# Gated mix of two attention blocks: the order of a pass over four rounds, with five bursts of V products

## The chip, the cores and the metric

The kernel runs on one core of a Trainium2 chip. The metric is device time in microseconds, the median of repeated executions of the same program. A profiled execution gives, beside its time, a trace with every instruction's engine, line, start and length. PE is the matrix engine (TensorE; its weight loads are listed as PEld), DVE is VectorE, ACT is ScalarE, POOL is GpSimd, and SP issues most of the transfers.

## The reference

Two attention blocks A and B read the same x (2048 tokens, 512 features). Each has 32 heads of 16 features and is a full softmax over 2048 keys. Their results are mixed by a gate per token. All inputs are float32.

```python
qkv = (x @ wqkv) -> q, k, v of 32 heads with Dh = 16
scores = einsum("bhqd,bhkd->bhqk", q, k) * (Dh ** -0.5)
p = softmax(scores)
o = einsum("bhqk,bhkd->bhqd", p, v) -> (2048, 512) @ wo

g = sigmoid((x * gate_w).sum(-1))
return g * A(x) + (1 - g) * B(x)
```

So there are 64 heads in all, each with a 2048 x 2048 matrix of scores, which is where the time goes.

## The kernel before

A prologue projects x to q, k and v, splits q and k into a high and a low part, and leaves them in DRAM. The main loop then works in *rounds*: a round is one head and one block of 128 keys, so a head has 16 rounds (NT) and there are 1024 (ROUNDS). The order of all instructions is written out by hand; nothing reorders them (`manual_schedule`). Every engine takes its own instructions in the order in which the program names them.

For each round there are four kinds of work:

- `score(r, c)`, a step "e": a matmul of 128 keys by 512 queries (50 rows of q and k parts, the maximum of each query among them) into a bank of the PSUM pool `ps_st` (four banks), then an exponential on ACT into a quarter of the tile `p` of that round (pool `ppool`, three buffers). Four of them make a round.
- the maxima, 20 rounds ahead (NT + LEAD): `max_plain(m, c)`, a step "m", is a matmul of 128 queries by 512 keys into the pool `ps_m` (three banks) and a maximum over it on DVE. For every second round, `max_rise` ("D": a matmul into `ps_st` and a Relu on ACT) and later `max_pair` ("A": a matmul into `ps_m` and one DVE instruction that adds the rise and takes the maximum) do in one DVE pass what two plain steps would do.
- `attend_next(n)`, a digit in the string: a *burst* of V products. The unit is a quarter, 128 of the 512 query columns of each of the four chunks of `p`. `attend` issues four matmuls at a time, one for each chunk, each at its own 32 columns of the array, and they add up in the one bank `acc`. Each takes 128 x 17 weights (V and a column of ones, which gives the denominator). A burst that crosses a round's end is two calls. Behind the last round of a head ACT copies `acc` out (`ev`), and the next head's first product waits for that.
- once a head, `max_split` reduces the maxima over the four chunks on DVE (`mrow`) and splits them on POOL; `max_rows` transposes them on DVE (`mt`), sends them out by one DMA on SP (`md`) and back by two into two rows of the head's q, on which the first "e" of that head waits.

The score matmuls ("e", "m", "D", "A") use 48 or 50 of the array's rows, and the helper `rows()` puts them by turns on partitions 0 and 64, so that two run at a time. `turn[0] = 0` at each burst starts again with partition 0.

The order comes from one string for each pass over two rounds, `FULL`; the last 20 rounds, which have no maxima left to take, use `LATE`. Work that is due by round (loads of V and weights, normalising, projections of finished groups of heads) stands in `later`; a pass calls what is due in its two rounds before its string begins, and projections wait for the next burst. The bursts run 8 quarters, two rounds, behind the scores.

Of the kernel before, what the change touches and what calls it, by code (L numbers as in the profile page):

```python
# [37 lines left out]
NT = S // P  # L38
# [5 lines left out]
ROUNDS = NH * NT  # L44
LEAD = 4
# [6 lines left out]
def gated_mha(ctx: ExitStack, tc: tile.TileContext, xT, x, wqkv_a, wo_a, wqkv_b, wo_b, gate_w, out):  # L52
# [34 lines left out]
    def load_stacks(h, halves=HALVES):  # L87
        dma = nc.sync.dma_start
        s, hh = divmod(h, H)
        g, j = divmod(hh, HG)  # L90
        q, k = q_st[h % 3], k_st[h % 3]
        qs, ks, xs = qd[s][g], kd[s][g], xd[s][g]

        def pairs(t, step, n=S):
            v = t[0, j]
            return bass.AP(tensor=v.tensor, offset=v.offset, ap=[[n, DH], [step, 2], [1, n]])

        for b in halves:
            dma(k[b:b + 32].bitcast(F32), pairs(ks, HG * DH * S))
            dma(q[b:b + 32].bitcast(F32), pairs(qs, 0))  # L100
            dma(k[b + 32:b + 48].bitcast(F32), ks[0, j])
            dma(q[b + 32:b + 48].bitcast(F32), qs[1, j])
        if h and halves[-1] == HALVES[1]:
            x = x_st[h % 2]
            dma(x[:32].bitcast(F32), pairs(xs, HG * DH * 512, 512))
            dma(x[32:SC].bitcast(F32), xs[0, j])
# [3 lines left out]


    LOWEST = -3.4028234e38
    FIRST = NT + LEAD + 2
    mxp, rises = {}, {}
    turn = [0]

    def rows():
        turn[0] ^= 1
        return HALVES[1 - turn[0]]

    def scores_bank(m, c):
        h, t = divmod(m, NT)
        if h not in mxp:
            mxp[h] = small.tile([P, NT, 4], F32, name="mxp")
            if h:
                pool.memset(mxp[h][:, FIRST % NT if h == 1 else 0::2, 1:2], LOWEST)
        pool_ = ps_st if c == "rise" else ps_m
        ps = pool_.tile([P, 512], F32, name="ps_st" if c == "rise" else "ps_m")
        b = rows()
        q = q_st[h % 3]  # L130
        if c == "rise":
            assert b == 0
            k = x_st[h % 2][:]
        else:
            k = k_st[h % 3][b:b + SC, c * 512:(c + 1) * 512]
        pe.matmul(ps, q[b:b + SC, t * P:(t + 1) * P], k, start=True, stop=True)  # L136
        return ps, mxp[h][:, t]

    def max_plain(m, c):
        ps, o = scores_bank(m, c)  # L140
        dve.tensor_reduce(o[:, c:c + 1], ps, op=ALU.max, axis=AX.X)  # L141
# [3 lines left out]
    def max_rise(m):  # L145
        ps, _ = scores_bank(m, "rise")
        rises[m] = small.tile([P, 512], F32, name="rise")
        act.activation(rises[m], ps, AF.Relu)  # L148

    def max_pair(m):  # L150
        ps, o = scores_bank(m, 0)
        rise = rises.pop(m)
        dve.tensor_tensor_reduce(out=rise, in0=ps, in1=rise, scale=1.0, scalar=LOWEST,  # L153
                                 op0=ALU.add, op1=ALU.max, accum_out=o[:, 0:1])
# [3 lines left out]
    def max_split(h):  # L158
        parts = mxp.pop(h)
        m = small.tile([P, NT], F32, name="mrow")  # L160
        mp = small.tile([P, 2, NT], F32R, name="mparts")
        dve.tensor_reduce(m, parts, op=ALU.max, axis=AX.X)  # L162
        pool.tensor_copy(mp[:, 0], m)  # L163
        pool.tensor_tensor(mp[:, 1], m, mp[:, 0].bitcast(F32), op=ALU.subtract)
        mparts[h] = mp

    def max_rows(h):
        mt = small.tile([P, 32], F32, name="mt")
        dve.transpose(mt, mparts.pop(h).rearrange("p i t -> p (i t)").bitcast(F32))
        q = q_st[h % 3]  # L170
        r = md[h % 3]
        nc.sync.dma_start(r.rearrange("i (t a x) -> a (i t) x", a=4, x=32), mt)
        for b in HALVES:
            nc.sync.dma_start(q[b + SC:b + SC + 2].bitcast(F32), r)
# [13 lines left out]
    with tc.tile_pool(name="xs", bufs=1) as xs, tc.tile_pool(name="pro", bufs=2) as pro, \  # L188
# [97 lines left out]
        ahead = [(m, c) for m in range(NT + LEAD) for c in range(4)]  # L286
# [228 lines left out]
    later = {}  # L515
# [53 lines left out]
    def attend(r, qa, qb):  # L569
        h, kt = divmod(r, NT)  # L570
        v, j = vg[h // HG], h % HG
        p = pt[r]
        final = h == NH - 1
        a = kt % 4
        first, last = (a == 0, a == 3) if final else (kt == 0, kt == NT - 1)
        for c in range(NQ):
            pe.matmul(acc[32 * c:32 * c + 17, qa * P:qb * P], v[:, 4 * a + c if final else kt, j],  # L577
                      p[:, c * 512 + qa * P:c * 512 + qb * P], start=first and qa == 0, stop=last,
                      tile_position=(0, 32 * c), skip_group_check=True)
        if qb < 4:  # L580
            return
        del pt[r]
        if final and last:
            ev = work.tile([P, 512], F32, name="ev")
            act.copy(ev, acc)  # L585
            hi = work.tile([P, 512], F32R, name="ev_hi", tag="num")
            lo = work.tile([P, 512], F32R, name="ev_lo")
            pool.tensor_copy(hi, ev)
            pool.tensor_tensor(lo, ev, hi.bitcast(F32), op=ALU.subtract)
            tail[kt // 4] = (hi, lo)  # L590
        elif last:
            G, j = divmod(h, HG)
            ev = work.tile([P, 512], F32, name="ev")
            act.copy(ev, acc)
            nc.sync.dma_start(od[G][j].rearrange("c r t -> (c r) t"), ev)


    done = [0]

    def attend_next(n):  # L600
        while n:
            r, qa = divmod(done[0], 4)
            qb = min(4, qa + n)
            attend(r, qa, qb)
            done[0] += qb - qa
            n -= qb - qa

    def score(r, c):
        h, kt = divmod(r, NT)
        if c == 0:  # L610
            pt[r] = ppool.tile([P, S], F32, name="p")
        q, k = q_st[h % 3], k_st[h % 3]
        kk, cc = (4 * (kt % 4) + c, kt // 4) if h == NH - 1 else (kt, c)
        b = rows()
        ps = ps_st.tile([P, 512], F32, name="ps_st")
        pe.matmul(ps, k[b:b + SC + 2, kk * P:(kk + 1) * P], q[b:b + SC + 2, cc * 512:(cc + 1) * 512],  # L616
                  start=True, stop=True)
        act.activation(pt[r][:, c * 512:(c + 1) * 512], ps, AF.Exp, scale=SCALE)  # L618
# [1 line left out]

    FULL = "m3memeem3meAe2Dmeee"
    LATE = "e2ee2ee2ee2e"
    after = {}

    for r in range(0, ROUNDS, 2):
        h, kt = divmod(r, NT)
        projects = []
        for rr in (r, r + 1):  # L630
            for fn, a in later.pop(rr, ()):
                if fn is project_out:
                    projects.append(a)
                else:
                    fn(*a)
        if kt == 0 and h + 2 < NH:
            load_stacks(h + 2)
        m = r + NT + LEAD
        plain = [(m, 2), (m, 3)] + [(m + 1, c) for c in range(4)]
        scored = 0  # L640
        for step in FULL if m < ROUNDS else LATE:
            if step == "e":
                score(r + scored // 4, scored % 4)
                scored += 1
            elif step == "m":
                max_plain(*plain.pop(0))
            elif step == "D":
                if m + 2 < ROUNDS:
                    max_rise(m + 2)
            elif step == "A":  # L650
                if m in rises:
                    max_pair(m)
                else:
                    max_plain(m, 0)
                    max_plain(m, 1)
            else:
                for a in projects:
                    project_out(*a)
                projects = []
                turn[0] = 0  # L660
                if r:
                    attend_next(int(step))
                if scored > 2 and r in after:
                    max_rows(after.pop(r))
        m += 1
        if m < ROUNDS and m % NT == NT - 1:
            max_split(m // NT)
            after[r + 2] = m // NT
    attend_next(8)
    fill_only.append(True)  # L670
    for fn, *a in fill:
        fn(*a)
# [25 lines left out]
```

## Time and profile before

| | us |
|---|---|
| median of 3 runs | 2805.46 (2804.55 to 2805.68) |
| profiled execution | 2804.7 |
| its span | 2802.9 |
| PE busy | 2785.4 |
| ACT busy | 2419.9 |
| DVE busy | 2363.9 |
| POOL busy | 254.8 |

The main loop fills the span from about 350 us on. A row of the timeline has the start in us from the span's start, the length in us, the engine, the line, the operation, the tiles (out<-in) and a count where like instructions in a row are merged. The end of a matmul is modelled, so the distance between starts says more than a length. A row of a group has the busy time and the mean length in ns of one, and then the engine's idle time before them with what ended it.

### The profile page before, as it was taken

The page shows a single profiled execution, that of the slowest core. Times are in us where ns is not written, and L with a number is a line of the kernel's source. Part 1 is how long each engine was busy: PE and PEld are TensorE (multiplying, and loading weights), DVE is VectorE, ACT ScalarE, POOL GpSimd, SP SyncE. Part 2 cuts the span into 40 slices and gives each one's busy share as a digit, 9 for nine tenths or more (in the row PEclk, how much of TensorE's full clock was granted, in tenths as well). Part 3 has the DMA queues.
Part 4 walks back from the last instruction along what each step waited for, and adds up shares of the span by engine and source line. Part 5 has one row for each costly group of instructions (what it writes and reads, how often), then busy time and mean ns, then how long its engine had stood idle before and what let it go on. Part 6 is the DMA issues. An engine that isn't in the chain of part 4 may idle for free.

```text
span 2802.9 us, 65443 instructions
## 1 busy us (share of the span) xinstructions
PE 2785.4 (99%) x26176; PEld 1319.3 (47%) x26176; DVE 2363.9 (84%) x4399; ACT 2419.9 (86%) x4758; POOL 254.8 (9%) x456
## 2 busy tenths in 40 slices
PE   8999999999999999999999999999999999999998
PEld 6877444444444444444444445444444444444444
DVE  4145799999999999999999877899999999998884
ACT  3221699999999999999999977899999999998785
POOL 2010111110000000000100232000000001011201
PEclk9999999999999999999999999999999999999999
DMA  7673333333332233333432442332333333333302
GB/s 255 206 251 145 84 62 78 69 70 59 70 62 53 50 58 62 58 60 58 89 54 50 104 100 63 58 56 49 63 54 60 58 78 70 58 73 86 77 10 92
DMA packets 91125, 225.24 MB, mean 80 GB/s; under 512 B 24150, under 2 KB 34358, under 8 KB 78278
## 3 DMA queue, kind: packets, MB, share of 16 engines
q1 hardware_dynamic: 88262, 212.15, 33.9%
q0 software_dynamic: 2560, 8.91, 1.2%
q8 instruction: 206, 3.38, 0.6%
q14 instruction: 97, 0.79, 0.1%
HBM read 152.07 MB, written 68.94 MB: 79 GB/s over the span
## 4 chain that ended last, share of the span: by engine, by line
PE 97%; DMA 1%; ACT 1%; DVE 1%; issue 0%; SPq 0%; DVEq 0%
PE acc L577 38%; PE ps_m L136 25%; PE ps_st L616 13%; PE ps_st L136 8%; PE ps_pro L233 5%; PE ps_m L459 3%; PE ps_pro L265 3%; ACT p L618 1%; DMA raw<-in_xT 0%; DMA k_st<-kd 0%; DMA qd<-part 0%; DVE mxp L141 0%; PE ps_st L459 0%; PE ps_st L510 0%; PE ps_m L510 0%
## 5 line engine op out<-in xcount | busy, mean ns | idle before, releaser
L618 ACT ACTIVATE p<-ps_st 128x512 f32<-128x512 f32 x4096 | 2077.0, 625 | 88.5 <-PE ps_st L616 73.8
L141 DVE TENSOR_REDUCE mxp<-ps_m 128x1 f32<-128x512 f32 x3094 | 1957.3, 683 | 183.4 <-PE ps_st L616 130.1
L136 PE MATMUL ps_m<-k_st,q_st 48*128 48x512 f32 x3595 | 1359.7, 446 | 1.2 <-DVE mxp L141 0.4
L616 PE MATMUL ps_st<-q_st,k_st 50*128 50x512 f32 x4096 | 1218.1, 427 | 0.0
L577 PE MATMUL acc<-p,vg 128*17 128x384 f32 (+1 forms) x16368 | 1186.0, 384 | 2.9 <-ACT ev L585 2.0
L136 PEld LDWEIGHTS ps_m<-k_st,q_st 48*128 48x128 f32 x3595 | 610.9, 184 | 555.4 <-DVE mxp L141 480.8
L616 PEld LDWEIGHTS ps_st<-q_st,k_st 50*128 50x128 f32 x4096 | 618.9, 185 | 198.6 <-ACT p L618 179.4
L577 PEld LDWEIGHTS acc<-p,vg 128*17 128x17 f32 x16368 | 315.1, 96 | 422.8 <-issue 400.0
L153 DVE CUSTOM_DVE_ANT_0 rise<-ps_m,rise 128x512 f32<-128x512 f32 x501 | 341.4, 681 | 0.0
L148 ACT ACTIVATE rise<-ps_st 128x512 f32<-128x512 f32 x501 | 301.7, 602 | 36.6
L136 PE MATMUL ps_st<-x_st,q_st 48*128 48x512 f32 x501 | 249.1, 497 | 0.0
L163 POOL CAST mparts<-mrow 128x16 fp32r<-128x16 f32 x64 | 12.6, 197 | 2010.9 <-DVE mrow L162 2010.9
L136 PEld LDWEIGHTS ps_st<-x_st,q_st 48*128 48x128 f32 x501 | 91.8, 183 | 211.8 <-ACT p L618 211.4
L237 ACT CAST part<-ps_pro 128x1024 fp32r<-128x1024 f32 x32 | 32.5, 1014 | 134.6 <-PE ps_pro L233 113.5
L238 DVE TENSOR_TENSOR part<-ps_pro,part 128x1024 fp32r<-128x1024 f32 x32 | 39.2, 1225 | 100.8 <-ACT part L237 82.0
L459 PE MATMUL ps_m<-wo,ot 128*128 128x512 f32 (+1 forms) x354 | 91.0, 402 | 0.0
L268 ACT COPY v_st<-ps_pro 128x512 f32<-128x512 f32 x31 | 18.2, 587 | 77.8 <-PE ps_pro L265 74.1
L233 PE MATMUL ps_pro<-xh,whi 128*128 128x512 f32 x256 | 72.9, 404 | 8.5 <-ACT xh L219 8.1
L459 PEld LDWEIGHTS ps_m<-wo,ot 128*128 128x128 f32 (+1 forms) x354 | 64.0, 188 | 20.2 <-issue 3.9
L233 PE MATMUL ps_pro<-xh,wlo 128*128 128x512 f32 x256 | 69.5, 394 | 0.0
L233 PE MATMUL ps_pro<-xl,whi 128*128 128x512 f32 x256 | 69.3, 393 | 0.0
L233 PEld LDWEIGHTS ps_pro<-xh,whi 128*128 128x128 f32 x256 | 47.5, 190 | 24.8 <-ACT xh L219 11.3
(99 smaller groups left out, 808.4 us busy)
## 6 DMA issues: line engine op xcount, KB each, us to landing
k_st<-kd SPq DMA_DIRECT2D x128, 256.0 KB
q_st<-qd SPq DMA_DIRECT2D x128, 256.0 KB
qd<-part SPq DMA_DIRECT2D x32, 512.0 KB
kd<-part SPq DMA_DIRECT2D x32, 512.0 KB
k_st<-kd SPq DMA_DIRECT2D x128, 128.0 KB
q_st<-qd SPq DMA_DIRECT2D x128, 128.0 KB
od<-ev SPq DMA_DIRECT2D x63, 256.0 KB
vd<-v_st SPq DMA_DIRECT2D x32, 272.0 KB
```

The lines of the kernel that those rows point to most:

```text
L136: pe.matmul(ps, q[b:b + SC, t * P:(t + 1) * P], k, start=True, stop=True)
L141: dve.tensor_reduce(o[:, c:c + 1], ps, op=ALU.max, axis=AX.X)
L148: act.activation(rises[m], ps, AF.Relu)
L153: dve.tensor_tensor_reduce(out=rise, in0=ps, in1=rise, scale=1.0, scalar=LOWEST, op0=ALU.add, op1=ALU.max, accum_out=o[:, 0:1])
L233: pe.matmul(ps[:, c * 512:(c + 1) * 512], a[:, k], b[:, k], start=n == 0, stop=n == 3 * KC - 1)
L237: act.copy(pt[0], ps)
L238: dve.tensor_tensor(pt[1], ps, pt[0].bitcast(F32), op=ALU.subtract)
L265: pe.matmul(ps[:, :DM], a[:, k, o:o + P], b[:, k], start=n == 0, stop=n == 3 * KC - 1)
L459: pe.matmul(ps, ot[a][:n, slot, sl], wt[b][:n, g], start=G == groups[0] and i == 0, stop=G == groups[-1] and i == 2)
L577: pe.matmul(acc[32 * c:32 * c + 17, qa * P:qb * P], v[:, 4 * a + c if final else kt, j], p[:, c * 512 + qa * P:c * 512 + qb * P], start=fi ...
L616: pe.matmul(ps, k[b:b + SC + 2, kk * P:(kk + 1) * P], q[b:b + SC + 2, cc * 512:(cc + 1) * 512], start=True, stop=True)
L618: act.activation(pt[r][:, c * 512:(c + 1) * 512], ps, AF.Exp, scale=SCALE)
```

## The change

A pass now covers four rounds, and `FULL` is a string for four: 16 "e", 12 "m", 2 "A", 2 "D", and five bursts of 3, 4, 3, 3 and 3 quarters. Twice the old string had six bursts (3, 3, 2, 3, 3, 2). Both "D" stand at the end of the pass and are for the rounds m + 4 and m + 6, so two rises are kept until the next pass. The first "m" of a pass is the third of its round. What is due by round is still called every two rounds: for the third and fourth round of a pass it is called ahead of the ninth "e". The bursts now run 7 quarters behind, as in the first pass those ahead of the eighth "e" are left out. `max_split` no longer stands at the end of a pass; it follows the first burst of the next one, and `max_rows` the second. `LATE` is the old string twice.

```diff
-    FIRST = NT + LEAD + 2
+    FIRST = NT + LEAD + 4
...
-    FULL = "m3memeem3meAe2Dmeee"
-    LATE = "e2ee2ee2ee2e"
-    after = {}
-
-    for r in range(0, ROUNDS, 2):
+    FULL = "mme3emmeem4meeemAe3emmeeem3meeemA3DeD"
+    LATE = "e2ee2ee2ee2e" * 2
+    splits = {}
+
+    for r in range(0, ROUNDS, 4):
...
+        due(r)
         if kt == 0 and h + 2 < NH:
             load_stacks(h + 2)
         m = r + NT + LEAD
-        plain = [(m, 2), (m, 3)] + [(m + 1, c) for c in range(4)]
+        plain = [(m + i, c) for i in range(4) for c in range(2 - i % 2 * 2, 4)]
+        pairs = [m, m + 2]
+        ahead = [m + 4, m + 6]
         scored = 0
+        steps = [max_split, max_rows] if r in splits else []
         for step in FULL if m < ROUNDS else LATE:
             if step == "e":
+                if scored == 8:
+                    due(r + 2)
                 score(r + scored // 4, scored % 4)
...
-                if r:
+                if r or scored >= 8:
                     attend_next(int(step))
-                if scored > 2 and r in after:
-                    max_rows(after.pop(r))
-        m += 1
-        if m < ROUNDS and m % NT == NT - 1:
-            max_split(m // NT)
-            after[r + 2] = m // NT
-    attend_next(8)
+                if steps:
+                    steps.pop(0)(splits[r])
+        if m < ROUNDS and (m + 4) % NT == 0:
+            splits[r + 4] = m // NT
+    attend_next(4 * ROUNDS - done[0])
```

More of the change, by code (lines that the diff above doesn't have):

```diff
@@ L618, in score, with due @@
         act.activation(pt[r][:, c * 512:(c + 1) * 512], ps, AF.Exp, scale=SCALE)
-    FULL = "m3memeem3meAe2Dmeee"
-    LATE = "e2ee2ee2ee2e"
-    after = {}
-    for r in range(0, ROUNDS, 2):
+    FULL = "mme3emmeem4meeemAe3emmeeem3meeemA3DeD"
+    LATE = "e2ee2ee2ee2e" * 2
+    splits = {}
+    for r in range(0, ROUNDS, 4):
         h, kt = divmod(r, NT)
         projects = []
[L630 to L635, printed above, removed]
+        def due(first):
+            for rr in (first, first + 1):
+                for fn, a in later.pop(rr, ()):
+                    if fn is project_out:
+                        projects.append(a)
+                    else:
+                        fn(*a)
+        due(r)
         if kt == 0 and h + 2 < NH:
@@ L647, in gated_mha @@
             elif step == "D":
-                if m + 2 < ROUNDS:
-                    max_rise(m + 2)
+                mm = ahead.pop(0)
+                if mm < ROUNDS:
+                    max_rise(mm)
             elif step == "A":
-                if m in rises:
-                    max_pair(m)
-                else:
-                    max_plain(m, 0)
-                    max_plain(m, 1)
+                mm = pairs.pop(0)
+                if mm in rises:
+                    max_pair(mm)
+                else:
+                    max_plain(mm, 0)
+                    max_plain(mm, 1)
             else:
@@ L658, in gated_mha @@
                     project_out(*a)
-                projects = []
+                projects.clear()
                 turn[0] = 0
-                if r:
+                if r or scored >= 8:
                     attend_next(int(step))
-                if scored > 2 and r in after:
-                    max_rows(after.pop(r))
-        m += 1
-        if m < ROUNDS and m % NT == NT - 1:
-            max_split(m // NT)
-            after[r + 2] = m // NT
-    attend_next(8)
+                if steps:
[3 more added lines that the diff above has]
+    attend_next(4 * ROUNDS - done[0])
     fill_only.append(True)
```

## The prediction

> **What bounds the kernel now.** I read the page's busy shares and chain first, then busy time in a long steady stretch, then the timeline of one period, engine by engine.
>
> ```profile
> PE 2785.4 (99%) x26176; PEld 1319.3 (47%) x26176; DVE 2363.9 (84%) x4399; ACT 2419.9 (86%) x4758; POOL 254.8 (9%) x456
> ...
> PE 97%; DMA 1%; ACT 1%; DVE 1%; issue 0%; SPq 0%; DVEq 0%
> ...
> 1000.00:1600.00 600.00, 600.00 (x6160) 257.11 (x6158) 558.87 (x1062) 586.61 (x1170) 34.84 (x77) 1.00 0.35 67
> ```
>
> The chain lies on TensorE (PE). But in the steady stretch ScalarE (ACT) is busy 586.61 of 600 us, 98%, and VectorE (DVE) 93%, at a full clock (1.00). So a saving on PE counts only as far as ACT can follow: three engines are close to being the bound. One period of two rounds:
>
> ```profile
> 1399.88 0.84 PE L577 MATMUL acc<-p,vg 128*17 128x384 f32 x8
> 1400.65 0.50 PE L136 MATMUL ps_m<-k_st,q_st 48*128 48x512 f32 x1
> 1400.65 0.49 PE L616 MATMUL ps_st<-q_st,k_st 50*128 50x512 f32 x1
> 1400.99 0.39 PE L136 MATMUL ps_m<-k_st,q_st 48*128 48x512 f32 x1
> 1400.99 0.39 PE L616 MATMUL ps_st<-q_st,k_st 50*128 50x512 f32 x1
> 1401.22 0.39 PE L136 MATMUL ps_m<-k_st,q_st 48*128 48x512 f32 x1
> ...
> 1401.55 0.85 PE L577 MATMUL acc<-p,vg 128*17 128x128 f32 x16
> ...
> 1402.32 0.50 PE L136 MATMUL ps_m<-k_st,q_st 48*128 48x512 f32 x1
> ...
> 1402.99 0.63 PE L577 MATMUL acc<-p,vg 128*17 128x256 f32 x8
> ...
> 1403.55 0.49 PE L136 MATMUL ps_st<-x_st,q_st 48*128 48x512 f32 x1
> ...
> 1404.47 0.84 PE L577 MATMUL acc<-p,vg 128*17 128x384 f32 x8
> ```
> ```profile
> 1399.97 4.02 ACT L618 ACTIVATE p<-ps_st 128x512 f32<-128x512 f32 x8
> 1404.08 0.60 ACT L148 ACTIVATE rise<-ps_st 128x512 f32<-128x512 f32 x1
> ```
> ```profile
> 1401.18 2.48 DVE L141 TENSOR_REDUCE mxp<-ps_m 128x1 f32<-128x512 f32 x4 [0.30 <-PE ps_m L136]
> ```
> ```profile
> 1404.04 0.18 PEld L616 LDWEIGHTS ps_st<-q_st,k_st 50*128 50x128 f32 x1 [0.20 <-ACT p L618]
> ```
>
> Prices from these rows, by starts:
> - Score matmuls (e, m, D, A) run two at a time, on partitions 0 and 64. I call such a pair a slot. A stretch of three slots lasts 0.90 (1400.65 to 1401.55), of two 0.67 (1402.32 to 1402.99): 0.23 per further slot, and 0.21 fixed.
> - A burst of three quarters lasts 0.77, whether in one call (1399.88) or two (1401.55); one of two quarters lasts 0.56 (1402.99 to 1403.55). So 0.21 per quarter and 0.14 fixed. Bursts of 3, 3, 2 and stretches of 3, 2, 3 slots give 0.77 + 0.90 + 0.77 + 0.67 + 0.56 + 0.92 = 4.59 us, 1399.88 to 1404.47.
> - ACT: eight exponentials in 4.02, the last about 0.6 long: one per 0.49. DVE: four maxima in 2.48, the last 0.68 long: one per 0.60. Either starts 0.04 after its matmul ends (1403.55 + 0.49 to 1404.08).
> - A score bank is free 0.05 after the exponential that read it (ends 1399.97 + 4.02 = 1403.99; the load waits until 1404.04). There are four ps_st banks, so the fifth score from here on waits for the first exponential.
>
> What disturbs the clean period comes once a head:
>
> ```profile
> L162 DVE TENSOR_REDUCE mrow<-mxp x6: 220/220/223, 1003.8 to 1190.1; 128x16 f32<-128x64 f32 x6
> ...
> 1016.81 0.60 ACT L594 COPY ev<-acc 128x512 f32<-128x512 f32 x1
> ...
> 1018.24 0.49 PE L136 MATMUL ps_m<-k_st,q_st 48*128 48x512 f32 x1
> ...
> 1019.38 0.85 PE L577 MATMUL acc<-p,vg 128*17 128x128 f32 x16
> ...
> 1039.79 0.50 PE L136 MATMUL ps_st<-x_st,q_st 48*128 48x512 f32 x1
> ...
> 1040.49 0.47 PE L136 MATMUL ps_m<-k_st,q_st 48*128 48x512 f32 x1
> 1040.89 0.52 PE L577 MATMUL acc<-p,vg 128*17 128x384 f32 x4
> ```
>
> A head takes (1190.1 - 1003.8)/5 = 37.26 us, eight clean periods of 4.595 take 36.76, so 0.50 a head is lost. One loss is ACT's copy of the head's result: soon after it a stretch of three slots lasts 1.14 (1018.24 to 1019.38) for 0.90. The other is the change of head in the maxima: 1.10 (1039.79 to 1040.89), its last matmul starting 0.70 in where 0.57 is usual.
>
> **The change, part by part.** It works on four rounds at a time, in 251 passes; the last 20 rounds (e2ee2...) keep their order.
>
> *Term 1, PE alone.* The same 16 quarters and 32 score matmuls stand in five bursts (3, 4, 3, 3, 3) in place of six. The stretches between them, counted round the string, hold 6, 6, 7, 7, 6 matmuls. Two are odd, and as each burst restarts at partition 0, their last matmul has a slot to itself: 3 + 3 + 4 + 4 + 3 = 17 slots where there were 16. So 3 x 0.90 + 2 x 1.13 + 4 x 0.77 + 0.98 = 9.02, against 2 x 4.59 = 9.18. Saved: 0.16 x 251 = 40 us. The saved burst alone is worth 0.35, the added slot costs 0.23 of it.
>
> *Term 2, waits for banks.* ACT has 16 exponentials and 2 rises, 18 x 0.49 = 8.82 of 9.02, so it may idle 0.2 in a pass. I walked once round the string by the prices above, zero at the first burst of three. The first stretch after it (e m m e e m) runs 0.77 to 1.67; its exponentials end at 2.14, 2.63 and 3.12. The burst of four lasts until 2.65 and feeds ACT nothing. The next stretch's first exponential then ends at 3.78, not 3.61: ACT has idled 0.17. That stretch (m e e e m A e) ends at 3.79, exponentials at 3.78, 4.27, 4.76, 5.25. Burst until 4.56. In the stretch e m m e e e m the fourth e needs the bank whose exponential ends at 5.25, so it loads at 5.30 and runs 0.27 late. The lone m behind it had a slot of its own and covers most: the stretch ends at 5.73, 0.04 late. The stretches m e e e m A and D e D m m e each lose 0.04 in the same way (scores that wait for exponentials four before them). Together 0.13, so a clean pass lasts 9.15. Cost: 0.13 x 251 = 33 us. Bounds: nothing (PE's 9.02) and 0.20 (9.22, with the two odd stretches waiting 0.05 more in their first slots). I take 0.13, which the rows' prices give; walking the old string with them gives 4.59 and a fraction, as the trace has.
>
> The Trainium skill, TensorEngine Tiling, section PSUM Bottleneck, says that packing speeds up TensorE but not the emptying of PSUM, which may then be the limit. By that alone nothing would be gained, and the time would stay near 2805. ACT's 98% agrees that emptying is close to the limit, the 0.18 us that it can idle in two rounds (4.59 - 9 x 0.49) says that it isn't there yet. The rival called a wash, below, is the case in which the page's rule would hold.
>
> *Term 3, once a head.* The copy of acc costs ACT 0.49. In the new string it comes after the burst of four, ahead of the two odd stretches, where scores wait for ACT anyway: by the same walk 0.31 in place of about 0.25. max_split (L162, 0.25 of DVE with its wait) moves from the end of a pass to behind the first burst, after two maxima of the next pass. There DVE has idled 0.28 before its next maximum, so it costs nearly nothing where 0.2 was lost; if that idle time is not there, the 0.2 stays. The extra DMA waits of the first two maxima on a new head stay, about 0.05. In sum 0.36 a head for 0.50: 0.14 x 63 = 9 us gained.
>
> *Term 4, the maxima's way to the next head.* max_rows (transpose, one DMA out, two in, on SP) must land before the next head's first e.
>
> ```profile
> 1006.74 0.20 DVE L169 STREAM_TRANSPOSE mt<-mparts 128x32 f32<-128x32 f32 x1
> ...
> 1006.97 0.58 SPq L172 DMA_DIRECT2D md<-mt  x1
> 1008.99 0.52 SPq L174 DMA_DIRECT2D q_st<-md  x2
> ...
> 1013.61 0.50 PE L616 MATMUL ps_st<-q_st,k_st 50*128 50x512 f32 x1
> ...
> SPq L174 <- DMA md<-mt: 99.0, 64, 3.2
> ...
> L185 POOL DMA_DIRECT2D vg<-vd x32 | 24.5, 769 | 2.3 <-PE ps_st L616 1.6 <-PE ps_m L136 0.4 <-issue 0.3
> ```
>
> Before, 6.87 us lie between the transpose and that e. The chain takes 2.25 to the second pair of DMAs, and if these take as long as the first (1006.97 to 1008.99, 2.0) plus the second issue, about 4.6. In the new string the e comes before the first burst and the transpose a little later: 5.6 us by the walk. It still fits by 1 us. The longest wait for the first DMA (3.2, against 99.0/64 = 1.5) makes a chain of some 6.3: in a few heads 0.4 to 0.7 late, 2 us in all. On POOL the fourth load of a V group now stands ahead of the split's two operations, but its 0.77 us of issue is over before DVE hands over mrow. SP's order past these DMAs is the same.
>
> *No cost:* later() work is still called every two rounds, so projections keep their number; around them PE alone is the limit, and term 1 counts in full there (1 to 2 us more). Two rises kept over a pass fit their two buffers: the second is written after the second A has read it. The three p buffers also do: each round's quarters are multiplied at least a burst ahead of the e that overwrites them. One quarter less is left at the end (0.2).
>
> **Sum:** -40 + 33 - 9 + 2 - 2 = -16 us. The profiled execution took 2804.7 (span 2802.9), the median is 2805.46, 0.8 above: 2789 us.
>
> **The rivals.**
> - *PE alone sets the time.* If the four banks hide every wait, term 2 vanishes: 2789 - 33 = 2756. For it: no PE gap of note now. Against it: loads already wait for ACT, and 18 x 0.49 leaves 0.2. A tenth; half of term 2 gives 2772.
> - *A wash.* ACT takes what the saved burst gives: term 2 at its 0.20 end and term 3's gain lost, 2789 + 18 + 9 = 2816 at the worst, around 2800 to 2809 with part of it. For it: 98%. Two in ten.
> - *Slower through lone matmuls.* If one alone in its slot costs more than 0.23, each 0.03 us of it takes 0.03 x 2 x 251 = 15 us, the whole forecast; 0.10, what a stretch's first slot takes beyond a later one (0.34 for 0.23), gives 2789 + 50 = 2839. Against it: the late lone m at 1040.49 ends at 1040.96 and the burst starts 0.07 earlier, just as after a pair (1401.22 + 0.39 to 1401.55). One in ten.
> - *Slower through term 4.* If the chain takes 6.9, as long as it had room before, the first e of each head is 1.3 late: up to 63 x 1.3 = 80 us, 2869. It decides from a chain of 5.9. One in twenty.
>
> **How the numbers follow.** Forecast 0.55 (its own range 2780 to 2798), PE alone 0.10, a wash 0.20, slower 0.15. A difference of 0.2%, 5.6 us, is about what a measurement here can tell. Faster: 0.55 + 0.10 + the better part of a wash, 0.06 = 0.71. Within: 0.14. Slower: 0.15. The range leaves out the lower half of PE alone and most of the slower cases: 2774 to 2807.
>
> **What would show it.** Right: 9.15 between the like bursts of clean passes; the stretches of seven at 1.13 and 1.18; ACT busier than 98%; exponentials idle 0.1 to 0.2 after the burst of four; heads of 37.0 us. Wrong: stretches of seven above 1.2 with no load waiting for ACT (lone matmuls), PE waiting at the first e of a head (term 4), or a clean pass of 9.02.

## The result

| | us |
|---|---|
| before, median of 6 runs | 2805.61 (2804.55 to 2807.07) |
| after, median of 6 runs | 2824.79 (2815.82 to 2827.24) |
| ratio after/before | 1.0064, 95% interval 1.0054 to 1.0074 |
| profiled execution after | 2827.24, span 2825.5 |

The change made the kernel slower by 0.64%, where I had forecast 0.6% faster. The times of after scatter by 11 us, those of before by 2.5 us; the mean granted clock of TensorE over a run goes from 0.987 in the longest run of after to 0.993 in its shortest.

The page after has the same engine at the end of the chain, with 7% fewer matmul records:

```profile
PE 2800.8 (99%) x24344; PEld 1399.9 (50%) x24344; DVE 2401.6 (85%) x4399; ACT 2413.2 (85%) x4757; POOL 254.3 (9%) x456
```

**Where the time came from.** The load of the first "e" of a head's first round is a mark in both traces (L616 on PEld; the timeline of before is the first fence, that of after the second).

```profile
341.26 0.18 PEld L616 LDWEIGHTS ps_st<-q_st,k_st 50*128 50x128 f32 x1
...
490.40 0.18 PEld L616 LDWEIGHTS ps_st<-q_st,k_st 50*128 50x128 f32 x1
...
2735.52 0.19 PEld L616 LDWEIGHTS ps_st<-q_st,k_st 50*128 50x128 f32 x2 [0.42 <-ACT p L618]
```
```profile
344.49 0.18 PEld L616 LDWEIGHTS ps_st<-q_st,k_st 50*128 50x128 f32 x1
...
497.33 0.18 PEld L616 LDWEIGHTS ps_st<-q_st,k_st 50*128 50x128 f32 x1
...
2734.87 0.19 PEld L616 LDWEIGHTS ps_st<-q_st,k_st 50*128 50x128 f32 x2 [0.21 <-issue]
```

| mark | after minus before, us | gained or lost since the last mark |
|---|---|---|
| first e of head 1 | +3.2 | 3.2 lost |
| first e of head 5 | +6.9 | 3.7 lost |
| first e of head 63 | -0.7 | 7.6 gained |
| end of the span | +22.6 | 23.3 lost |

So 58 heads of the main loop did gain, and the last 16 rounds with what follows them lost three times as much. There the granted clock of TensorE (PEclk, the third number from the end of a row of busy time by stretch) is at half in after. In the fence below, the first row is of before:

```profile
2741.00:2795.00 54.00, 52.01 (x407) 28.10 (x399) 26.93 (x44) 30.34 (x61) 10.22 (x12) 1.00 0.27 100
```
```profile
2741.00:2795.00 54.00, 50.71 (x407) 16.88 (x399) 7.44 (x10) 32.29 (x60) 6.37 (x8) 0.50 0.12 41
```

The trace has one stretch of 54.6 us at half clock there, one of 13.7 us at the start of the main loop (before: 6.8) and one of 6.8 us from 457.7 us on. The timeline after, PE and then ACT, shows how the long one begins:

```profile
2737.28 0.63 PE L577 MATMUL acc<-p,vg 128*17 128x256 f32 x8
2737.84 0.49 PE L616 MATMUL ps_st<-q_st,k_st 50*128 50x512 f32 x2
2738.26 0.41 PE L577 MATMUL acc<-p,vg 128*17 128x128 f32 x8
2739.98 0.41 PE L577 MATMUL acc<-p,vg 128*17 128x128 f32 x8 [1.31 <-ACT ev L594]
...
2742.10 1.05 PE L577 MATMUL acc<-p,vg 128*17 128x128 f32 x16
2743.09 0.79 PE L616 MATMUL ps_st<-q_st,k_st 50*128 50x512 f32 x2
2743.81 1.05 PE L577 MATMUL acc<-p,vg 128*17 128x256 f32 x8
```
```profile
2736.89 2.57 ACT L618 ACTIVATE p<-ps_st 128x512 f32<-128x512 f32 x5
2739.34 0.59 ACT L594 COPY ev<-acc 128x512 f32<-128x512 f32 x1
```

In the last 20 rounds the bursts have two quarters. 7 quarters behind the scores, one of them takes the last quarter of a head and the first of the next (2738.26 and 2739.98). The second call needs `acc` empty, ACT has a backlog of exponentials before the copy, and PE does nothing for 1.31 us in the middle of the burst. 1.2 us after the gap's end the clock is at half: from one burst to the next it takes 1.71 us (2742.10 to 2743.81) where 0.98 was usual (2737.28 to 2738.26). Before, with a lag of 8 quarters, a head ended with a burst, the next two scores stood between it and the wait, and PE was idle for 0.88:

```profile
2738.92 0.63 PE L577 MATMUL acc<-p,vg 128*17 128x256 f32 x8
2739.48 0.50 PE L616 MATMUL ps_st<-q_st,k_st 50*128 50x512 f32 x2
2740.86 0.63 PE L577 MATMUL acc<-p,vg 128*17 128x256 f32 x8 [0.88 <-ACT ev L594]
```

The last head copies `acc` out every four rounds, so it has three more such waits: 1.1 us of idle PE each in after, 0.7 before.

The smaller loss near 457 us is a head's first "e" that waits for the maxima's rows, followed by 6.8 us at half clock (after, timeline of PE):

```profile
455.56 0.62 PE L136 MATMUL ps_m<-k_st,q_st 48*128 48x512 f32 x2
457.53 0.63 PE L616 MATMUL ps_st<-q_st,k_st 50*128 50x512 f32 x1 [1.35 <-DMA q_st<-md]
```

**The main loop after.** One clean pass, the starts of its stretches and bursts (timeline of PE, after):

```profile
1036.48 0.50 PE L136 MATMUL ps_st<-x_st,q_st 48*128 48x512 f32 x1
...
1037.42 0.84 PE L577 MATMUL acc<-p,vg 128*17 128x384 f32 x8
1038.19 0.50 PE L616 MATMUL ps_st<-q_st,k_st 50*128 50x512 f32 x1
...
1039.09 1.05 PE L577 MATMUL acc<-p,vg 128*17 128x512 f32 x8
1040.08 0.50 PE L136 MATMUL ps_m<-k_st,q_st 48*128 48x512 f32 x1
...
1041.21 0.84 PE L577 MATMUL acc<-p,vg 128*17 128x384 f32 x8
1041.98 0.49 PE L616 MATMUL ps_st<-q_st,k_st 50*128 50x512 f32 x1
...
1043.19 0.84 PE L577 MATMUL acc<-p,vg 128*17 128x128 f32 x16
1043.96 0.49 PE L136 MATMUL ps_m<-k_st,q_st 48*128 48x512 f32 x1
...
1044.92 0.85 PE L577 MATMUL acc<-p,vg 128*17 128x256 f32 x16
1045.69 0.50 PE L136 MATMUL ps_st<-x_st,q_st 48*128 48x512 f32 x1
```

The stretches last 0.94, 0.90, 1.13, 1.21 and 0.96, the pass 9.21 us (1036.48 to 1045.69), against 9.19 for two clean periods before.

### The profile page after: what moved, and what is told of

It reads as the page before. It is cut to its first block, busy times and chain, and to the rows that moved or that the text cites. A ratio compares the mean times of both kernels' runs of the same rounds, so it can differ in the third digit from the quotient of the medians.

```text
span 2825.5 us, 61766 instructions
## 1 busy us (share of the span) xinstructions
PE 2800.8 (99%) x24344; PEld 1399.9 (50%) x24344; DVE 2401.6 (85%) x4399; ACT 2413.2 (85%) x4757; POOL 254.3 (9%) x456
## 4 chain that ended last, share of the span: by engine, by line
PE 95%; DMA 2%; DVE 1%; ACT 1%; issue 0%; SPq 0%; DVEq 0%
PE acc L577 37%; PE ps_st L616 22%; PE ps_m L136 20%; PE ps_st L136 5%; PE ps_pro L233 5%; PE ps_m L459 3%; PE ps_pro L265 3%; DVE mxp L141 1%; DMA md<-mt 1%; DMA raw<-in_xT 1%; ACT p L618 0%; DMA k_st<-kd 0%; DMA q_st<-md 0%; DMA qd<-part 0%; PE ps_st L459 0%
## 5 line engine op out<-in xcount | busy, mean ns | idle before, releaser
L618 ACT ACTIVATE p<-ps_st 128x512 f32<-128x512 f32 x4096 | 2104.3, 636 | 128.2 <-PE ps_st L616 67.1
L616 PE MATMUL ps_st<-q_st,k_st 50*128 50x512 f32 x4096 | 1316.7, 443 | 3.2 <-DMA q_st<-md 2.8
L136 PE MATMUL ps_m<-k_st,q_st 48*128 48x512 f32 x3596 | 1226.3, 439 | 1.2 <-DVE mxp L141 0.6
L577 PE MATMUL acc<-p,vg 128*17 128x128 f32 (+3 forms) x14536 | 1152.7, 416 | 4.6 <-ACT ev L585 3.3
L616 PEld LDWEIGHTS ps_st<-q_st,k_st 50*128 50x128 f32 x4096 | 620.7, 186 | 475.1 <-ACT p L618 399.7
L136 PEld LDWEIGHTS ps_m<-k_st,q_st 48*128 48x128 f32 x3596 | 603.6, 185 | 381.3 <-DVE mxp L141 320.1
L577 PEld LDWEIGHTS acc<-p,vg 128*17 128x17 f32 x14536 | 292.5, 97 | 418.2 <-issue 346.3
L136 PE MATMUL ps_st<-x_st,q_st 48*128 48x512 f32 x500 | 182.8, 445 | 0.0
L136 PEld LDWEIGHTS ps_st<-x_st,q_st 48*128 48x128 f32 x500 | 73.8, 185 | 52.8 <-issue 52.8
L459 PE MATMUL ps_m<-wo,ot 128*128 128x512 f32 (+1 forms) x354 | 90.6, 401 | 1.2
```

Source lines behind the costliest of these rows:

```text
L459: pe.matmul(ps, ot[a][:n, slot, sl], wt[b][:n, g], start=G == groups[0] and i == 0, stop=G == groups[-1] and i == 2)
```

## The experiments

My theory after the result: the lag of 7 quarters lets heads end inside bursts in the last 20 rounds, PE's gap there drops the clock, and the half clock is what costs (theory 1). The rival: the new main loop loads PE less, so the clock falls at the end whatever the last rounds do (theory 2).

**late_aligned**: one digit of the changed kernel.

```diff
-        for step in FULL if m < ROUNDS else LATE:
+        late = "e1" + LATE[2:] if m == ROUNDS else LATE
+        for step in FULL if m < ROUNDS else late:
```

> The changed kernel, but the first burst of the last 20 rounds has 1 quarter in place of 2, so that these rounds run 8 quarters behind again and a head ends at the end of a burst. Theory 1 (the new lag of 7 quarters lets a head end inside a burst there, PE waits for ACT's copy of acc in mid-burst, and the granted clock stays at half for 55 us): the 23 us lost after 2735 us come back, 2800 to 2805 us, no stretch at half clock after 2700. Theory 2 (the new main loop loads PE less, and the clock falls at the end whatever the last rounds do): 2818 or more, half clock stays at the end.

Measured: 2803.39 us (2800.07 to 2804.9), ratio to before 0.9994 (0.9984 to 1.0003). The same 54 us, in this run:

```profile
2741.00:2795.00 54.00, 52.01 (x391) 29.66 (x392) 29.12 (x48) 27.61 (x56) 10.84 (x12) 1.00 0.27 95
```

From head 63's first e to the end it takes 66.9 us, before 67.4, after 90.6. One quarter at the start of the last rounds gives back the whole loss there.

**before_late_shift**: the reverse, in the kernel before.

```diff
-        for step in FULL if m < ROUNDS else LATE:
+        late = "e3" + LATE[2:] if m == ROUNDS else LATE
+        for step in FULL if m < ROUNDS else late:
...
-    attend_next(8)
+    attend_next(4 * ROUNDS - done[0])
```

> The kernel before, whole, but the first burst of its last 20 rounds has 3 quarters in place of 2, so that these rounds run 7 quarters behind. Theory 1: slower by 15 to 25 us (2820 to 2830), half clock for tens of us after 2735. Theory 2: no change beyond 1 us, clock at full.

Measured: 2826.34 us (2816.43 to 2829.53), ratio 1.0069 (1.0049 to 1.0089), with the old main loop untouched:

```profile
2741.00:2795.00 54.00, 49.94 (x409) 17.08 (x412) 6.89 (x10) 33.15 (x62) 6.51 (x8) 0.51 0.13 42
```

The wait in mid-burst is there too (timeline of PE):

```profile
2739.83 0.41 PE L577 MATMUL acc<-p,vg 128*17 128x128 f32 x8
2741.78 0.41 PE L577 MATMUL acc<-p,vg 128*17 128x128 f32 x8 [1.53 <-ACT ev L594]
```

This is the loss of the change without the change. Theory 2 falls.

**early_rows**: the changed kernel, the split and the rows of the maxima one burst earlier.

```diff
-        steps = [max_split, max_rows] if r in splits else []
+        steps = [max_rows] if r in splits else []
...
         if m < ROUNDS and (m + 4) % NT == 0:
+            max_split(m // NT)
             splits[r + 4] = m // NT
```

> The changed kernel with max_split back at the end of a pass and max_rows behind the first burst of the next one, so that the maxima's rows start for the next head about 1.5 us earlier. The waits of some heads' first e for the rows (0.6 to 1.8 us, in six heads, the first of them with 6.8 us at half clock) go: 6 to 10 us less than the changed kernel, if the last rounds behave the same; the loss in the last 20 rounds stays, so 2814 to 2820. If the split on DVE costs more at this place, 3 us less of it.

Measured: 2823.57 us (2811.96 to 2826.34), ratio 1.0054 (1.0037 to 1.0072): 1 us below the changed kernel by the medians, whose scatter hides the effect. In its trace the first e of head 4 loads at 455.31, in after's at 457.50, and the stretch of half clock there is gone. A miss as a time; as a place in the trace it holds.

**both**: the two edits together.

> Both edits. Theory 1: the sum of both, 2792 to 2797 us, faster than the kernel before by 8 to 13 us. Theory 2: 2810 or more.

Measured: 2800.13 us (2798.92 to 2804.34), ratio 0.9983 (0.9974 to 0.9993), faster than before, by less than expected. Against late_aligned, which scatters less than early_rows, the earlier rows are worth 3.3 us.

**late_busy**: does the gap cost, or the clock? The changed kernel with work that nobody reads in the gap.

```diff
+    def idle_products(n):
+        for _ in range(n):
+            ps = ps_m.tile([P, 512], F32, name="ps_m")
+            b = rows()
+            pe.matmul(ps, k_st[1][b:b + SC, :P], q_st[1][b:b + SC, :512], start=True, stop=True)
...
+            ends = 4 if r >= ROUNDS - NT else NT
+            if n and done[0] > 4 * (ROUNDS - 24) and (r + 1) % ends == 0 and qb == 4:
+                turn[0] = 0
+                idle_products(12)
+                turn[0] = 0
```

> The changed kernel; where a burst of the last 20 rounds crosses a head's end (four places), PE gets 12 more score matmuls between the two calls, about 1.4 us of work that nobody reads, while it waits for ACT's copy of acc. Theory 1 (the gap in PE's work drops the clock, and the half clock is what costs): the clock stays full after 2735 us, the time falls by 15 to 22 us against the changed kernel, to 2803 to 2810. Rival (the waits in mid-burst cost by themselves): no gain or a loss of up to 3 us, since the waits stay as long, 2820 to 2830.

Measured: 2809.09 us (2802.97 to 2810.86), ratio 1.0012 (1.0002 to 1.0021), 15.7 below the changed kernel. The gap is filled (timeline of PE; L604 is the added work) and the clock holds, although the added work outlasts the wait: the two calls start 2.68 us apart, where they started 1.72 apart in after.

```profile
2737.39 0.41 PE L577 MATMUL acc<-p,vg 128*17 128x128 f32 x8
2737.73 2.40 PE L604 MATMUL ps_m<-q_st,k_st 48*128 48x512 f32 x12
2740.07 0.41 PE L577 MATMUL acc<-p,vg 128*17 128x128 f32 x8
```
```profile
2741.00:2795.00 54.00, 54.00 (x531) 31.23 (x524) 22.00 (x36) 30.50 (x61) 10.20 (x12) 1.00 0.21 76
```

From head 63's first e to the end: 73.6 us. So of the 23 us that the last rounds lost, at least 17 are the half clock (90.6 - 73.6). The 6 that late_busy still loses are the waits in mid-burst and the added work itself, which holds the second call back by about 1 us (2.68 - 1.72) at the first of the four places.

**start_busy**: is the half clock at the start of the main loop due to the bursts that the first pass leaves out? In the run with both edits, each of the two got 8 score matmuls that nobody reads in its place (`idle_products(8)` where `attend_next` is skipped).

> Both edits (last rounds 8 quarters behind, maxima's rows early), and in the first pass, where two bursts are left out, 8 score matmuls that nobody reads stand in the place of each. If PE's idle time in the first pass holds the clock at half there for 13 to 17 us in place of 7 to 10, the clock is full after 310 us and the time 2 to 3 us below that of both edits (2797 to 2798). If the first pass is slow for another reason, it is the same or 1 to 2 us slower (2800 to 2802).

Measured: 2805.66 us (2803.78 to 2808.37), ratio 1.0003 (0.9993 to 1.0012): 5.5 us worse than both and outside either expectation, with 20.5 us at half clock at the start. The added work takes time itself, and it did not raise the clock there.

**old_start**: the run with both edits, its first pass in the old order.

```diff
+        full = "m3memeem3meAe2Dmeee" * 2 if r == 0 else FULL.replace("3", "4", 1) if r == 4 else FULL
-        for step in FULL if m < ROUNDS else late:
+        for step in full if m < ROUNDS else late:
```

> Both edits, and the first pass of four rounds runs in the old order (six bursts, two odd stretches less); the second pass begins with a burst of 4 in place of 3, from where all is as in the run with both edits. If the new order of the first passes is what keeps the clock at half for 13 to 17 us there, it is at half for 7 to 10 us as before, and the time is 2 to 3 us below both edits: 2797 to 2798. If the start has nothing to do with the order, 2800 and 13 us or more at half clock.

Measured: 2798.77 us (2794.99 to 2800.59), ratio 0.9976 (0.9967 to 0.9986), the lowest median of the versions that leave nothing out. The first 17 us from 303 on, in after and then in this run:

```profile
303.00:320.00 17.00, 16.81 (x96) 6.98 (x96) 12.02 (x21) 10.44 (x21) 1.12 (x2) 0.60 0.67 123
```
```profile
303.00:320.00 17.00, 16.79 (x106) 6.99 (x106) 13.95 (x24) 12.32 (x24) 0.45 (x2) 0.80 0.63 110
```

A mean clock of 0.80 is 6.8 us at half, as before; 0.60 is 13.7. The length varies between traces of the same order, but it goes with the order: 6.8 to 10.2 us with the old one (before, before_late_shift, old_start), 13.7 to 17.1 with the new one (six traces). What that is worth in time is not shown clearly: the medians of both and old_start lie 1.4 us apart, less than either scatters. Why the new order holds the clock down longer stays open.

**no_rise**: is the second stretch of seven long because ACT is nearly full? The run with both edits, without the D steps; the maxima then leave out the second chunk of keys, and A adds zero.

```diff
     def max_rise(m):
-        ps, _ = scores_bank(m, "rise")
-        rises[m] = small.tile([P, 512], F32, name="rise")
-        act.activation(rises[m], ps, AF.Relu)
+        rises[m] = None
...
```

> Both edits, without the two D steps of a pass (no rise is computed and the max over the second chunk of keys is left out; A adds zero), so ACT has 16 evictions in a pass and not 18. PE alone: 2 x 0.90 + 2 x 1.13 + 0.67 + 4.06 = 8.79 us a pass. If the stretches of seven are long because scores wait for ACT's banks (1.21 for the second), they fall to 1.13 to 1.15 both, the stretches of six to 0.90, and a clean pass is 8.8 to 8.9. If a lone matmul is dear by itself, the second stretch of seven stays at 1.2 and the pass is 8.95 or more.

Measured, one run: 2749.66 us, clean passes of 8.98 to 9.04 us, and the second stretch of seven still at 1.21. By the expectation that speaks for dear lone matmuls. The trace says otherwise (load on PEld, then ACT):

```profile
1031.68 0.18 PEld L618 LDWEIGHTS ps_st<-q_st,k_st 50*128 50x128 f32 x1 [0.25 <-ACT p L620]
1031.69 0.18 PEld L136 LDWEIGHTS ps_m<-k_st,q_st 48*128 48x128 f32 x1
```
```profile
1029.57 3.53 ACT L620 ACTIVATE p<-ps_st 128x512 f32<-128x512 f32 x7 [0.74 <-PE ps_m L136]
```

The fourth "e" of that stretch waits for ACT as before, and the lone "m" loads right behind it. ACT was idle for 0.74 us during the burst of four; its four next exponentials, one per 0.49 from 1029.57 on, set when the bank comes free. So the wait comes from ACT running dry in the long burst, not from ACT's mean load, and two evictions less in the pass do not remove it. My expectation had not separated these two.

## Why the prediction was wrong

- **The step that failed** is the sentence that the last 20 rounds "keep their order", which costed them at nothing, and with it "one quarter less is left at the end (0.2)". Their string is the same, but its bursts start one quarter on. That moves the head's end into a burst, and the wait for ACT's copy with it, from 0.88 to 1.31 us of idle PE. I looked for that wait in the new string (term 3) and not in the old one under the new lag. It cost 23 us, all of which came back with one quarter less in the first of these bursts (late_aligned): at least 17 by the clock, which no rival had.
- **Term 4** was the right mechanism, too small: 2 us in a few heads, where the first e of six heads came 0.6 to 1.7 us late, the latest with 6.8 us at half clock after it. Taking it away gave 3.3 us (both against late_aligned). The room for the chain was as worked out: 5.62 us from transpose to first e in most heads, 5.6 predicted.
- **The start** had no term: 3.2 us by head 1. About 2 of them go with the order of the first pass and its longer half clock: from the first e of head 0 to that of head 1 it is 43.3 us in both and 41.0 in old_start.
- **Terms 1 and 2** hold in their mechanism. The stretches came out at 0.94, 0.90, 1.13, 1.21, 0.96 for 0.94, 0.90, 1.13, 1.18, 0.94, no lone matmul was dear, and the fourth "e" of the second stretch of seven was late (its load, after's trace, ended by ACT):

```profile
1042.76 0.18 PEld L616 LDWEIGHTS ps_st<-q_st,k_st 50*128 50x128 f32 x1 [0.25 <-ACT p L618]
```

  Term 2 was mis-sized: most clean passes take 9.19 or 9.20, so about 0.18 of waits and not 0.13, near the bound that I had given to the wash. Behind the burst of four two exponentials start 0.74 apart (1039.90 and 1040.64, ACT, after) where 0.48 is usual, so ACT loses 0.26 there and not 0.17. The waits are all that PE saved: a clean pass took 9.19 before and takes 9.19 or 9.20 after.
- **Term 3** was right in sign and larger: passes of an ordinary head are 9.20, 9.20, 9.20 and 9.47 us, so 0.27 a head is lost beside the clean passes, where I had 0.36 and before had 0.50. An ordinary head takes 37.08 us, predicted 37.0, before 37.26, and all of that gain is this term's. That the head came out so near 37.0 is partly luck, as a pass was longer than I had it (by 0.05) and the loss beside the passes smaller (by 0.09).
- **No gain around the projections** beyond this: heads there went from 49.0 to 48.8 us, where I had counted term 1 in full.
- The main loop alone therefore gained about 10 us (0.18 x 57), not 18, and the version that keeps it while mending the rest (old_start) is 0.24% faster than before.

Of the page's rule on PSUM in TensorEngine Tiling (the Trainium skill, section PSUM Bottleneck), the traces bear out that emptying the banks takes back what TensorE saves: 0.18 us of waits in a clean pass for 0.16 saved. They add where: behind the burst in which ACT gets nothing to empty.

## What to carry to other kernels

When a lag between two streams changes, walk every section that uses it, the tail and the first pass too, and look for the waits that the new phase puts in the middle of a run of work. A tail whose text is unchanged is not unchanged. And price a new gap on TensorE not by its length alone: look at the granted clock in the stretch behind it.

## What the runs showed of the hardware

- In a loop that is otherwise full, a gap on PE of 1.31 us (after, early_rows), 1.35 (after) or 1.53 (before_late_shift) was followed by a half clock within 1.2 us of its end. The longest gaps there without a drop were 1.01 us (late_aligned, up to 458.04) and 1.06 us (late_busy, up to 758.78).
- The stretches at half clock come in steps of 3.41 us: all that end before their span does last 2 to 6 steps (6.8 to 20.5 us) or 16 (54.6). In after, the second and the third begin 45 and 714 steps behind the first. Each of the four gaps that were followed by a drop lies whole in the step that the drop ended. So where a gap falls in such a step may count beside its length; no run here tests that.
- Once at half, the clock stayed there for 54.6 us in the traces of after, early_rows and before_late_shift, with PE idle only in three waits of 1.1 us. It came back 0.6 and 0.3 us behind the start of the closing projections in the first two and 0.2 us ahead of it in the third, so it is not shown that they brought it back. Nor is this length fixed: a mean clock of 0.993 in the shortest run of after means some 39 us at half in the whole run (an estimate, 2 x 0.007 x 2814), where the profiled one had 75. The Trainium skill, TensorE: Matmul & The Clock Gate, section Why this matters for your kernels, warns of idle gaps of more than about 3 us, and its first part has the clock back after some 3.4 us of sustained work. Here both differ: a shorter gap was enough, and almost 14 us of work without any gap (between two of the waits of 1.1 us) were not; the measurement decides. The two states that this page of the Trainium skill lists, one half and full, agree with 0.50 and 1.00 here.
- What holds the clock up stays open: score matmuls on 48 rows, two at a time, did not raise it at the start (start_busy), yet work of the same kind held it in the tail (late_busy).
